# An attention and feed-forward kernel: the summaries of batches 1 to 3 turn their weights in blocks on VectorE, with one maximum for four chunks

## The chip, the core and the metric

The kernel runs on one core of a Trainium2 chip, as one launch. Its time is device microseconds of that core. Besides TensorE (matmuls and turns through the array), VectorE, ScalarE and GpSimd do the arithmetic, and SyncE (SP) issues nearly all transfers, in the order of its own queue.

## The reference

`x` is 4 batches of 12,480 tokens with 128 channels, `inducing` 32 rows of 128 channels, all in single precision. Per batch:

```python
def mab(q, kv):
    s = scale * (q @ kv.transpose(0, 2, 1))      # scale = 1/sqrt(128)
    s = s - s.max(-1, keepdims=True)
    a = np.exp(s)
    a /= a.sum(-1, keepdims=True) + 1e-09
    return a @ kv
h = mab(I, x)          # the summary: 32 rows attend to 12,480 tokens
y = mab(x, h)          # every token attends to those 32 rows
# then, for all 49,920 tokens:
t = y @ w_in           # 128 -> 2048
g = where(t >= 1, t, where(t <= -1, 0, (t + 1)**2 / 4))
out = g @ w_out        # 2048 -> 128
```

## The kernel before

A batch is cut into 26 chunks of 480 tokens. For every chunk, `chunk` makes the 2048 hidden rows in eight steps of two 128-row halves: TensorE writes them to PSUM (line 953), ScalarE takes relu(t+1) (line 961) and then its square over 4 (line 947), VectorE the smaller of that and max(t, 1) (line 966). In six of eight steps the result is split into a rounded part `hi` and a rest `lo`, and TensorE adds three products (line 1053); `hi` is made by VectorE, ScalarE or GpSimd, whichever the plan picks, and `lo` by GpSimd (line 1027). In the other two one product in full precision does. VectorE turns the chunk's output (line 1065), and SP stores it in four pieces.

Before a batch's chunks can start, its 32 summary rows must be known. `summarize(b)` makes them. Batch 0's runs at the start, with nothing beside it; those of batches 1 to 3 run beside the chunks of the batch before. A summary works on groups of four chunks: six full ones and one of two. For a group of batches 1 to 3:

- `load` fetches `xn`, 120 partitions by 4 rows of tokens for each chunk, from a pool of nine buffers, and `xr`, the same tokens in 32-wide pieces, which VectorE turns into `xT` (channels by tokens).
- `score`: four matmuls, one for each chunk, write to the four 32-row quadrants of one PSUM bank (line 554): row 32q + m has the scores of summary row m with the tokens of chunk q. VectorE takes each row's maximum (line 559) and its multiple by -scale (line 562), ScalarE the exponentials with their sum (line 571). The bank is held from the first of these steps to the last.
- `gather`: TensorE turns the weights, four transposes of 120 tokens each, into another bank (line 595); ScalarE or VectorE copies them to `eN` (line 603). Then 16 matmuls (line 611) weigh the tokens: quadrant q of the output takes weights and tokens of chunk q only, so each quadrant stands under its own maximum. ScalarE keeps the result in `hs` (line 618).

After the last group, small steps bring the 28 partial sums of each summary row under one maximum, and add them with matmuls over `hs` (line 694). The maxima and sums of each group and quadrant stand in `mg` and `sg`.

All work is put in order by a planner in the file, `Plan.order`. Each operation is added with an engine or a choice of engines, a cost and a lag in nanoseconds, and a due time; the plan runs a clock, and whenever an engine is free it takes the operation that could start and is due first. The operations are then issued in that order, so each engine and SP's queue have a fixed order. Buffers, PSUM banks among them (pool `h`, seven banks), are given out by the plan as well. `DUE`, `LONE`, `KEEP` and `WAIT` are its constants: `LONE` puts off an operation whose twin (the other half of a step) isn't ready, since both halves in neighbouring banks can be done by one wide operation.

Of the kernel before, what the change touches and what calls it, by code (L numbers as in the profile page):

```python
# [9 lines left out]
F32 = mybir.dt.float32  # L10
# [3 lines left out]
ALU = mybir.AluOpType  # L14
# [9 lines left out]
SLOTS = dict(  # L24
    h=7, o=1, xn=9, xT=26, xr=2, e1=1, eN=1, hw=6, hx=1, hy=1, w=8, hi=4, lo=4, aT=3, s2=2, a=1, ahi=1, oT=1
)

FIRST = ["xn", "w", "xn", "hi", "xn", "w", "xn", "lo", "xn", "w"]

# [3 lines left out]
DUE = {  # L33
# [17 lines left out]
    "end": [-102350],  # L51
# [18 lines left out]

LONE = {"r": 7750, "t": 3200}

KEEP = 100

WAIT = 175250

# [176 lines left out]
def attn_moe(  # L253
# [29 lines left out]

    SHAPE = [(5, 96)] + [(4, 120)] * (B - 1)
    x_first = x.rearrange("b (k p t) c -> b k p t c", p=96, t=5)
    x_rows = x.rearrange("b (k t p) c -> b k p t c", p=120, t=4)
# [3 lines left out]
    FORM = dict(  # L290
        xn=([96, 5, C], F32), xT=([C, CW], F32),
        xr=([C, NB, M], F32), e1=([P, CW], F32), eN=([96, 5, P], F32), hw=([P, 512], F32R), hx=([P, 512], F32R), hy=([P, 512], F32R),
        w=([P, 2, CW], F32), hi=([P, 2, CW], F32R), lo=([P, 2, CW], F32R), aT=([P, CW], F32R),
        s2=([P, NB, M], F32), a=([P, CW], F32), ahi=([P, CW], F32R), oT=([C, NB, M], F32),
    )
    banks = psum.tile([P, SLOTS["h"] + SLOTS["o"], 512], F32, name="banks")
    count = [0]

    def make(slot, shape=None, dtype=None):

        count[0] += 1
        if slot.pool in ("h", "o"):
            slot.tile = banks[:, slot.place + (SLOTS["h"] if slot.pool == "o" else 0), :]
            return slot.tile
# [17 lines left out]
    def in_turn(pool, near=None):  # L322
        turns[pool] += 1
        return Slot(pool, turns[pool] - 1, near)
# [162 lines left out]
    def summarize(b, begin, pace, end):  # L487

        xn, got, e1, eN = {}, {}, {}, {}
        T, TP = SHAPE[b]  # L490
        rows_of = x_rows if b else x_first
        lasts, mosts, summed = [], [], []
        prior = state.get("chain")

        def load(g, due, step):
            for q in range(nqs[g]):
                c = g * Q + q
                due += step
                xT[b, c] = in_turn("xT")

                pool = FIRST[c % len(FIRST)] if b == 0 else "xn"
                xn[c] = in_turn(pool) if pool == "xn" else Slot(pool)
                got[c] = add(
                    "SP", 700 if b else 1000, 3000 if b else 5800, at(due, "x") if b else at(0, "x0", c),
                    lambda c=c: nc.sync.dma_start(make(xn[c], [TP, T, C], F32), rows_of[b, c]), [], [xn[c]],
                )
                got_all[b, c] = got[c]
                if b == 0:
                    pt = Slot("h")

                    def turn(c=c, pt=pt):
                        p = make(pt)
                        for t in range(T):
                            nc.tensor.transpose(  # L514
                                p[:, t * TP : (t + 1) * TP], xn[c].tile[:, t, :], ident[:TP, :TP]
                            )

# [25 lines left out]
        def score(g, due):  # L543

            nq = nqs[g]
            rows = nq * M
            cs = [g * Q + q for q in range(nq)]
            p1, e1[g] = Slot("h"), Slot("e1")
            nb = small("nb", [P, 1], f"_{b}_{g}")

            def scores():
                p = make(p1)
                for q, c in enumerate(cs):
                    nc.tensor.matmul(  # L554
                        p[q * M : (q + 1) * M, :CW], indT, xT[b, c].tile, start=True, stop=True
                    )

            def most():
                nc.vector.tensor_reduce(
                    mg[:rows, g : g + 1], p1.tile[:rows, :CW], axis=AX.X, op=ALU.max  # L560
                )
# [16 lines left out]
            v = add("DVE", 760, 900, SC[1], most, [m, folded, prior], [p1])  # L578
            mosts.append(v)
            e = add("ACT", 645, 780, SC[2], exps, [v], [e1[g], p1])  # L580
            summed.append(e)
            return e

        def gather(g, due, scored):
# [3 lines left out]
            pe, pf, ph, eN[g] = Slot("h"), Slot("h"), Slot("h"), Slot("eN")  # L588
            to = [pe, pf] if b == 0 else [pe]

# [9 lines left out]
            def put():  # L600
                copy = nc.scalar.copy if v.engine == "ACT" else nc.vector.tensor_copy
                e = make(eN[g], [TP, T, P], F32)
                copy(e[:, :4, :rows], pe.tile[:TP].rearrange("p (t w) -> p t w", w=P)[:, :, :rows])  # L603
                if b == 0:
                    copy(e[:, 4, :rows], pf.tile[:TP, :rows])

# [12 lines left out]

            GA = [at(due, "GA", n) for n in range(4)] if b else [at(0, "g0", g)] * 4  # L620
# [3 lines left out]
            by = dict(DVE=(615, 750, when), ACT=(485, 620, when))  # L624
            if b == 0:
                by = dict(ACT=(660, 800, when) if nq == Q else (430, 570, when))
            v = add(by, 0, 0, 0, put, [m], [eN[g], *to])
# [510 lines left out]
```

## Time and profile before

| | us |
|---|---|
| median of 3 runs | 1732.59 (1731.34 to 1733.43) |
| profiled execution | 1732.11 |
| its span, first to last instruction | 1730.3 |
| TensorE busy (matmuls) | 1696.6 |
| ScalarE busy | 1664.2 |
| VectorE busy | 1626.2 |
| GpSimd busy | 1612.6 |

Busy time is the time in which at least one instruction of the engine ran. A matmul's end is modelled, so a busy TensorE may still have room. The granted clock of TensorE was 0.999 of full speed. A row of groups reads: line, engine, operation, what it writes and reads, shapes, count, then busy time, mean duration, and idle time before.

### The profile page before, as it was taken

The numbers are of one execution on the slowest core, as the hardware profiler recorded it, in microseconds if no ns is written. First come the engines' busy times: TensorE is split into PE (matmuls) and PEld (weight loads), VectorE is DVE, ScalarE is ACT, GpSimd is POOL, SyncE is SP. The second block draws the span as 40 slices with busy tenths as digits, with TensorE's granted clock in tenths as the row PEclk, the third lists the DMA queues.
The fourth block names the chain that finished last, engine by engine and source line by source line (L and its number), as shares of the span: only waits on it lengthen the run. The fifth ranks groups of instructions, "written<-read, shape, count | busy, mean of one in ns | idle before, by whom it ended". The sixth has DMA issues, their size and how long they took to land.

```text
span 1730.3 us, 26049 instructions
## 1 busy us (share of the span) xinstructions
PE 1696.6 (98%) x8062; PEld 1229.5 (71%) x8062; DVE 1626.2 (94%) x2167; ACT 1664.2 (96%) x2486; POOL 1612.6 (93%) x875
## 2 busy tenths in 40 slices
PE   6999999999999999999999999999999999999998
PEld 5667777777767777777777777777777677777776
DVE  5799999999999999999999999999999999999997
ACT  5699999999999999999999999999999999999997
POOL 1599999999899999999999999999989999999997
PEclk9999999999999999999999999999999999999999
DMA  9443323333334233343143333232212111111111
GB/s 235 112 74 69 74 58 70 57 62 61 70 66 77 47 72 63 66 75 68 31 93 54 74 68 69 51 66 52 42 34 53 33 30 30 35 35 35 33 31 18
DMA packets 427950, 105.76 MB, mean 61 GB/s; under 512 B 370562, under 2 KB 421218, under 8 KB 427810
## 3 DMA queue, kind: packets, MB, share of 16 engines
q1 hardware_dynamic: 426722, 103.84, 30.5%
q8 instruction: 64, 1.05, 0.3%
q14 instruction: 76, 0.62, 0.1%
q10 hardware_dynamic: 1088, 0.25, 0.1%
HBM read 48.94 MB, written 25.56 MB: 43 GB/s over the span
## 4 chain that ended last, share of the span: by engine, by line
PE 62%; ACT 16%; DVE 11%; issue 5%; POOL 3%; DMA 2%; SPq 1%; DVEq 0%; ACTq 0%; POOLq 0%
PE banks L1053 43%; PE banks L953 14%; ACT w L961 8%; ACT w L947 6%; DVE w L966 6%; DVE hi L1024 3%; POOL lo L1027 2%; PE banks L611 1%; PE banks L765 1%; ACT hi L1021 1%; PE banks L554 1%; SPq L532 1%; DMA xr<-in_x 1%; DVE oT L1065 1%; PE banks L514 1%
## 5 line engine op out<-in xcount | busy, mean ns | idle before, releaser
L1027 POOL TENSOR_TENSOR lo<-w,hi 128x960 fp32r<-128x960 f32 x623 | 1395.9, 2271 | 40.3 <-DVE hi L1024 17.9
L966 DVE SCALAR_TENSOR_TENSOR w<-banks,w 128x480 f32<-128x480 f32 (+1 forms) x1200 | 960.6, 838 | 35.9 <-ACT w L947 30.7
L961 ACT ACTIVATE w<-banks 128x480 f32<-128x480 f32 (+1 forms) x1352 | 843.7, 700 | 15.0 <-PE banks L953 13.9
L947 ACT ACTIVATE w<-w 128x960 f32<-128x960 f32 x832 | 842.2, 1049 | 2.7
L953 PE MATMUL banks<-aT,hw 128*128 128x480 f32 x1664 | 605.6, 432 | 7.3 <-DVE w L966 5.2
L1053 PE MATMUL banks<-hi,w_lo 128*128 128x480 f32 x1246 | 492.0, 395 | 5.4 <-DVE oT L1065 3.3
L1024 DVE TENSOR_REDUCE hi<-w 128x960 fp32r<-128x960 f32 x409 | 464.7, 1142 | 18.2 <-PE banks L1053 1.2
L1053 PE MATMUL banks<-hi,w_hi 128*128 128x480 f32 x1246 | 472.9, 380 | 0.0
L953 PEld LDWEIGHTS banks<-aT,hw 128*128 128x128 f32 x1664 | 304.7, 188 | 167.6 <-DVE w L966 71.1
L1053 PE MATMUL banks<-w,w_f 128*128 128x480 f32 x836 | 391.4, 567 | 0.0
L1053 PE MATMUL banks<-lo,w_hi 128*128 128x480 f32 x1246 | 385.2, 395 | 0.8 <-POOL lo L1027 0.8
L1053 PEld LDWEIGHTS banks<-hi,w_lo 128*128 128x128 f32 x1246 | 234.2, 188 | 76.2 <-DVE oT L1065 18.0
L1053 PEld LDWEIGHTS banks<-lo,w_hi 128*128 128x128 f32 x1246 | 229.8, 188 | 76.2 <-POOL lo L1027 25.7
L1053 PEld LDWEIGHTS banks<-hi,w_hi 128*128 128x128 f32 x1246 | 234.2, 188 | 40.0 <-issue 7.2
L1053 PEld LDWEIGHTS banks<-w,w_f 128*128 128x128 f32 x836 | 155.9, 189 | 68.7 <-issue 50.9
L1019 POOL TENSOR_SCALAR hi<-w 128x960 fp32r<-128x960 f32 x140 | 139.6, 1002 | 19.3 <-DVE w L966 10.4
L1021 ACT CAST hi<-w 128x960 fp32r<-128x960 f32 x74 | 75.5, 1021 | 4.7 <-DVE w L966 3.1
L1065 DVE STREAM_TRANSPOSE oT<-banks 128x480 f32<-128x480 f32 x104 | 70.1, 674 | 7.9 <-PE banks L1053 6.5
L535 DVE STREAM_TRANSPOSE xT<-xr 128x480 f32<-128x480 f32 x78 | 51.2, 659 | 0.0
L808 POOL TENSOR_TENSOR a<-a,ahi 128x480 fp32r<-128x480 f32 (+1 forms) x28 | 34.5, 1232 | 0.6 <-ACT ahi L805 0.6
L441 POOL TENSOR_TENSOR w_in_sb<-hi,lo 128x256 f32<-128x256 f32 x8 | 6.1, 763 | 28.4 <-DVE hi L430 28.4
L611 PEld LDWEIGHTS banks<-xn,eN 120*32 120x32 f32 (+1 forms) x754 | 24.4, 109 | 11.1 <-ACT eN L603 4.4
(107 smaller groups left out, 580.0 us busy)
## 6 DMA issues: line engine op xcount, KB each, us to landing
out<-oT SPq DMA_DIRECT2D x414, 60.0 KB, 2.2
xn<-in_x SPq DMA_DIRECT2D x91, 240.0 KB, 4.2
xr<-in_x SPq DMA_DIRECT2D x312, 60.0 KB, 2.5
aT<-ahi SPq DMA_DIRECT2D x206, 60.0 KB, 2.0
aT<-a SPq DMA_DIRECT2D x206, 60.0 KB, 2.0
w<-in_moe_w_in SPq DMA_DIRECT2D x8, 256.0 KB, 5.7
w<-in_moe_w_out SPq DMA_DIRECT2D x8, 256.0 KB, 3.8
hw<-hy SPq DMA_DIRECT2D x32, 64.0 KB, 2.0
```

Of the source, the lines that this page charges most:

```text
L535: nc.vector.transpose(make(xT[b, c]), xr.tile.rearrange("c n i -> c (n i)"))
L611: nc.tensor.matmul(p[q * M : (q + 1) * M, :C], eN[g].tile[:, t, q * M : (q + 1) * M], xn[g * Q + q].tile[:, t, :], start=(t == 0), stop=(t ...
L947: nc.scalar.activation(w.tile, w.tile, AF.Square, scale=0.5)
L953: nc.tensor.matmul(make(h)[:, :CW], hw[b][ft // 4].tile[:, ft % 4 * P : (ft % 4 + 1) * P], aT[b, c].tile, start=True, stop=True,)
L961: each(of, i, hs_, lambda h, to: nc.scalar.activation(to, h, AF.Relu, bias=1.0), w)
L966: lambda h, t: nc.vector.scalar_tensor_tensor(h if kept else t, h, 1.0, t, op0=ALU.max, op1=ALU.min), w,
L1019: nc.gpsimd.tensor_scalar(make(hi), w.tile, 1.0, 0.0, op0=ALU.mult, op1=ALU.add)
L1021: nc.scalar.copy(make(hi), w.tile)
L1024: nc.vector.tensor_reduce(make(hi), w.tile.unsqueeze(3), axis=AX.X, op=ALU.max)
L1027: nc.gpsimd.tensor_sub(make(lo), w.tile, hi.tile.bitcast(F32))
L1053: nc.tensor.matmul(acc.tile[:, :CW], wt[k][:, i, :], g.tile[:, i, :], start=first, stop=(acc.parts == 0),)
L1065: nc.vector.transpose(make(oT).rearrange("c n i -> c (n i)"), acc.tile[:, :CW])
```

## The change

For batches 1 to 3 alone:

- The tokens for weighing are loaded like `xr`'s, 32 partitions by 15 consecutive tokens for a chunk, and the four chunks of a group share one buffer, a quadrant each. The buffers are three, of 15 x 128 columns over all partitions; batch 0 uses the same memory as nine buffers of 96 partitions. The first load of a later batch waits for the weighing of batch 0.
- The maximum of each row goes to `mq`; four transfers bring the four quadrants' maxima side by side on 32 partitions, VectorE takes the maximum over them, and four transfers write it to all quadrants of `mg`. So the four chunks stand under one maximum.
- The exponentials are written in the order in which the scores lie.
- Instead of TensorE's turns and the copy, one VectorE instruction turns all 32 x 32 blocks of `e1` into `eN`. Block n then has, for every quadrant, 32 tokens by 32 summary rows.
- 15 matmuls weigh the tokens, each over the 128 partitions of the four chunks together; matmul n adds to quadrant n % 4.

Batch 0 keeps its instructions. All due times but those of the weights and of batch 0's loads, turns, scores and weighing are new, and so are `LONE`, `KEEP` and `WAIT`.

```diff
-LONE = {"r": 7750, "t": 3200}
-KEEP = 100
-WAIT = 175250
+LONE = {"r": 6200, "t": 800}
+KEEP = 800
+WAIT = 210850
...
+                    xn[c] = xn[c - 1] if q else in_turn("xn")
+                    def fetch(c=c, q=q):
+                        t = xn[c].tile or make(xn[c])
+                        nc.sync.dma_start(t[q * M : (q + 1) * M], x_cols[b, c])
+                    got[c] = add("SP", 700, 3000, at(due, "x"), fetch, state["first"], [xn[c]])
...
             def most():
-                nc.vector.tensor_reduce(
-                    mg[:rows, g : g + 1], p1.tile[:rows, :CW], axis=AX.X, op=ALU.max
-                )
+                to = mq[:rows] if b else mg[:rows, g : g + 1]
+                nc.vector.tensor_reduce(to, p1.tile[:rows, :CW], axis=AX.X, op=ALU.max)
+                if b == 0:
+                    less()
+            def line(q):
+                nc.sync.dma_start(m4[:, q : q + 1], mq[q * M : (q + 1) * M])
+            def one_most():
+                nc.vector.tensor_reduce(m4[:, Q:], m4[:, :nq], axis=AX.X, op=ALU.max)
+            def spread(q):
+                nc.sync.dma_start(mg[q * M : (q + 1) * M, g : g + 1], m4[:, Q:])
+            def less():
                 nc.vector.tensor_scalar(nb[:rows], mg[:rows, g : g + 1], -SCALE, None, op0=ALU.mult)
...
-                    to = make(e1[g])[:rows].rearrange("w (i n) -> w i n", i=M)
-                    of = p1.tile[:rows, :CW].rearrange("w (n i) -> w i n", i=M)
+                    to, of = make(e1[g])[:rows], p1.tile[:rows, :CW]
...
+                l = [add("SP", 610, 2700, SC[1], lambda q=q: line(q), [v]) for q in range(nq)]
+                v = add("DVE", 75, 215, SC[1], one_most, l)
+                l = [add("SP", 610, 2700, SC[1], lambda q=q: spread(q), [v, prior]) for q in range(Q)]
+                mosts.extend(l)
+                v = add("DVE", 75, 215, SC[1], less, l)
...
+            if b:
+                def over():
+                    to = make(eN[g], [P, NB, M])[:rows].rearrange("p n m -> p (n m)")
+                    nc.vector.transpose(to, e1[g].tile[:rows])
+                def weigh_all():
+                    p = make(ph)
+                    for n in range(NB):
+                        nc.tensor.matmul(
+                            p[n % Q * M : (n % Q + 1) * M, :C], eN[g].tile[:rows, n, :], xn[g * Q].tile[:rows, n, :],
+                            start=n < Q, stop=n >= NB - Q,
+                        )
+                def keep_all():
+                    nc.scalar.copy(hs[:, g, :], ph.tile[:, :C])
+                v = add("DVE", 600, 735, GA[1], over, [scored], [e1[g], eN[g]])
+                m = add("PE", 880, 1080, GA[2], weigh_all, [v, *(got[g * Q + q] for q in range(nq))],
+                        [ph, eN[g], xn[g * Q]], tiled=True)
+                lasts.append(add("ACT", 150, 290, GA[3], keep_all, [m, folded, prior], [ph]))
+                return
```

## Rows read from the trace of the kernel before

**Rows 1.** The page's head and engine table: busy us, share of the span.

```profile
span 1730.3 us, 26049 instructions
PE 1696.6 (98%) x8062; PEld 1229.5 (71%) x8062; DVE 1626.2 (94%) x2167; ACT 1664.2 (96%) x2486; POOL 1612.6 (93%) x875
```

**Rows 2.** The page's chain that ended last, by engine.

```profile
PE 62%; ACT 16%; DVE 11%; issue 5%; POOL 3%; DMA 2%; SPq 1%; DVEq 0%; ACTq 0%; POOLq 0%
```

**Rows 3.** Stretches between output turns, line 1065 alone: stretch, us, VectorE busy (count), clock.

```profile
932.60:1345.20 412.60, 17.52 (x26) 1.00 0.29 56
1345.20:1725.00 379.80, 16.88 (x25) 1.00 0.16 31
```

**Rows 4.** Stretches, all engines: us, then PE, PEld, DVE, ACT, POOL busy.

```profile
93.90:516.00 422.10, 417.39 (x1947) 300.41 (x1947) 404.41 (x523) 416.04 (x613) 407.37 (x220) 1.00 0.35 66
516.00:932.60 416.60, 414.52 (x1934) 300.18 (x1933) 399.03 (x523) 410.08 (x611) 402.04 (x216) 1.00 0.34 65
932.60:1345.20 412.60, 410.54 (x1914) 298.70 (x1913) 393.95 (x513) 406.38 (x601) 396.76 (x210) 1.00 0.29 56
1345.20:1725.00 379.80, 376.65 (x1524) 273.67 (x1523) 364.78 (x451) 372.29 (x539) 369.95 (x192) 1.00 0.16 31
```

**Rows 5.** Groups of one summary, by shape, from 500 to 900 us.

```profile
L611 PE MATMUL banks<-xn,eN 120*32 120x128 f32 x208 | 7.6, 276 | 0.0
L554 PE MATMUL banks<-xT,indT 128*32 128x480 f32 x52 | 7.1, 578 | 0.0
...
L571 ACT ACTIVATE e<-banks,nb 128x480 f32<-128x480 f32 x6 | 4.1, 683 | 0.0
L802 DVE STREAM_TRANSPOSE a<-s 128x480 f32<-128x480 f32 x6 | 4.0, 670 | 0.4 <-POOL s L797 0.4
...
L595 PE MATMUL banks<-ident,e 128*120 128x128 f32 x24 | 3.6, 272 | 0.0
...
L603 ACT COPY eN<-banks 120x512 f32<-120x512 f32 x4 | 2.5, 614 | 0.0
...
L694 PE MATMUL banks<-ff,hs 128*128 128x32 f32 x14 | 1.7, 264 | 0.0
L603 DVE COPY eN<-banks 120x512 f32<-120x512 f32 x2 | 1.4, 687 | 0.3 <-PE banks L595 0.3
...
L720 PE MATMUL banks<-w_in_sb,hT 128*32 128x512 f32 x8 | 1.1, 604 | 0.0
...
L595 PE MATMUL banks<-ident,e 64*120 64x64 f32 x4 | 0.4, 230 | 0.0
L603 DVE COPY eN<-banks 120x256 f32<-120x256 f32 x1 | 0.4, 425 | 0.4 <-PE banks L595 0.4
...
L653 DVE TENSOR_REDUCE m<-mg 128x1 f32<-128x7 f32 x1 | 0.1, 144 | 0.0
```

**Rows 6.** Timeline of one group's scores, exponentials and turns: start us, us, what.

```profile
588.66 1.01 PE L554 MATMUL banks<-xT,indT 128*32 128x480 f32 x8
...
593.10 2.61 SPq L1069 DMA_DIRECT2D out<-oT  x4
...
595.38 0.68 ACT L571 ACTIVATE e<-banks,nb 128x480 f32<-128x480 f32 x1
...
597.86 0.60 PE L595 MATMUL banks<-ident,e 128*120 128x128 f32 x4
...
598.22 0.68 PE L953 MATMUL banks<-aT,hw 128*128 128x480 f32 x2
...
600.56 0.68 DVE L603 COPY eN<-banks 120x512 f32<-120x512 f32 x1
```

**Rows 7.** Line 831, the pieces of aT: us from issue to landing.

```profile
DMA to landing us min/median/max: 1.9/2.0/3.8
```

**Rows 8.** What SP's queue waited for: us in total, times, longest us.

```profile
SPq L1069 <- DVE oT L1065: 381.9, 51, 12.3
```

**Rows 9.** Waits of the engines: us in total, times, longest us.

```profile
PEld banks L953 <- DVE w L966: 71.1, 221, 1.7
```

More of the change, by code (lines that the diff above doesn't have):

```diff
@@ L24 @@
 SLOTS = dict(
-    h=7, o=1, xn=9, xT=26, xr=2, e1=1, eN=1, hw=6, hx=1, hy=1, w=8, hi=4, lo=4, aT=3, s2=2, a=1, ahi=1, oT=1
+    h=7, o=1, xn=3, x3=9, xT=26, xr=2, e1=1, eN=1, hw=6, hx=1, hy=1, w=8, hi=4, lo=4, aT=3, s2=2, a=1, ahi=1, oT=1
 )
-FIRST = ["xn", "w", "xn", "hi", "xn", "w", "xn", "lo", "xn", "w"]
+FIRST = ["x3", "w", "x3", "hi", "x3", "w", "x3", "lo", "x3", "w"]
 STEP = 1950
 DUE = {
[17 rows of a table removed]
-    "end": [-102350],
[17 rows of a table added]
+    "end": [-87250],
     "wi": [-503600, -107150, -99300, -322650, -80150, -599500, -48900, 17550],
@@ L280, in attn_moe @@
     psum = ctx.enter_context(tc.tile_pool(name="psum", bufs=1, space=bass.MemoryType.PSUM))
-    SHAPE = [(5, 96)] + [(4, 120)] * (B - 1)
+    T, TP = 5, 96
     x_first = x.rearrange("b (k p t) c -> b k p t c", p=96, t=5)
-    x_rows = x.rearrange("b (k t p) c -> b k p t c", p=120, t=4)
     x_cols = x.rearrange("b (k i n) c -> b k i n c", i=M, n=NB)
@@ L290, in attn_moe @@
     FORM = dict(
-        xn=([96, 5, C], F32), xT=([C, CW], F32),
+        xT=([C, CW], F32),
         xr=([C, NB, M], F32), e1=([P, CW], F32), eN=([96, 5, P], F32), hw=([P, 512], F32R), hx=([P, 512], F32R), hy=([P, 512], F32R),
@@ L296, in attn_moe @@
     banks = psum.tile([P, SLOTS["h"] + SLOTS["o"], 512], F32, name="banks")
+    tokens = work.tile([P, SLOTS["xn"], 3 * 5 * C], F32, name="tokens")
     count = [0]
@@ L303, in make @@
             slot.tile = banks[:, slot.place + (SLOTS["h"] if slot.pool == "o" else 0), :]
+            return slot.tile
+        if slot.pool == "xn":
+            slot.tile = tokens[:, slot.place, :].rearrange("p (n c) -> p n c", n=NB)
+            return slot.tile
+        if slot.pool == "x3":
+            n, k = divmod(slot.place, 3)
+            slot.tile = tokens[:TP, n, k * T * C : (k + 1) * T * C].rearrange("p (t c) -> p t c", t=T)
             return slot.tile
@@ L489, in summarize @@
         xn, got, e1, eN = {}, {}, {}, {}
-        T, TP = SHAPE[b]
-        rows_of = x_rows if b else x_first
         lasts, mosts, summed = [], [], []
         prior = state.get("chain")
+        state.setdefault("first", lasts)
         def load(g, due, step):
@@ L499, in load, with fetch @@
                 xT[b, c] = in_turn("xT")
[L501 to L505, printed above, removed]
-                )
+                if b == 0:
+                    pool = FIRST[c % len(FIRST)]
+                    xn[c] = in_turn(pool) if pool == "x3" else Slot(pool)
+                    def fetch(c=c):
+                        nc.sync.dma_start(make(xn[c], [TP, T, C], F32), x_first[b, c])
+                    got[c] = add("SP", 1000, 5800, at(0, "x0", c), fetch, [], [xn[c]])
+                else:
+                    xn[c] = xn[c - 1] if q else in_turn("xn")
[3 more added lines that the diff above has]
+                    got[c] = add("SP", 700, 3000, at(due, "x"), fetch, state["first"], [xn[c]])
                 got_all[b, c] = got[c]
@@ L513, in turn @@
                         for t in range(T):
-                            nc.tensor.transpose(
-                                p[:, t * TP : (t + 1) * TP], xn[c].tile[:, t, :], ident[:TP, :TP]
-                            )
+                            nc.tensor.transpose(p[:, t * TP : (t + 1) * TP], xn[c].tile[:, t, :], ident[:TP, :TP])
                     def put(c=c, pt=pt):
@@ L549, in score @@
             nb = small("nb", [P, 1], f"_{b}_{g}")
+            mq, m4 = small("mq", [P, 1], f"_{b}_{g}"), small("m4", [M, Q + 1], f"_{b}_{g}")
             def scores():
@@ L577, in score @@
                     [p1, e1[g], *(xT[b, c] for c in cs)], tiled=True)
-            v = add("DVE", 760, 900, SC[1], most, [m, folded, prior], [p1])
-            mosts.append(v)
+            v = add("DVE", 760 if b == 0 else 690, 900, SC[1], most, [m, folded, prior], [p1])
+            if b == 0:
+                mosts.append(v)
+            else:
+                l = [add("SP", 610, 2700, SC[1], lambda q=q: line(q), [v]) for q in range(nq)]
[3 more added lines that the diff above has]
+                v = add("DVE", 75, 215, SC[1], less, l)
             e = add("ACT", 645, 780, SC[2], exps, [v], [e1[g], p1])
@@ L588, in gather @@
             pe, pf, ph, eN[g] = Slot("h"), Slot("h"), Slot("h"), Slot("eN")
-            to = [pe, pf] if b == 0 else [pe]
+            if b:
[11 more added lines that the diff above has]
+                    nc.scalar.copy(hs[:, g, :], ph.tile[:, :C])
+                GA = [at(due, "GA", n) for n in range(4)]
+                v = add("DVE", 600, 735, GA[1], over, [scored], [e1[g], eN[g]])
[3 more added lines that the diff above has]
+                return
+            to = [pe, pf]
             def turn():
@@ L603, in put @@
                 copy(e[:, :4, :rows], pe.tile[:TP].rearrange("p (t w) -> p t w", w=P)[:, :, :rows])
-                if b == 0:
-                    copy(e[:, 4, :rows], pf.tile[:TP, :rows])
+                copy(e[:, 4, :rows], pf.tile[:TP, :rows])
             def weigh():
@@ L618, in keep @@
                 nc.scalar.copy(hs[:rows, g, :], ph.tile[:rows, :C])
-            GA = [at(due, "GA", n) for n in range(4)] if b else [at(0, "g0", g)] * 4
+            GA = [at(0, "g0", g)] * 4
             each_ = 110 if nq == Q else 85
@@ L623, in gather @@
             when = GA[1]
-            by = dict(DVE=(615, 750, when), ACT=(485, 620, when))
-            if b == 0:
-                by = dict(ACT=(660, 800, when) if nq == Q else (430, 570, when))
+            by = dict(ACT=(660, 800, when) if nq == Q else (430, 570, when))
             v = add(by, 0, 0, 0, put, [m], [eN[g], *to])
```

2 lines of the change are left out of this document (1 added, 1 removed), and 48 rows, old and new, of the table DUE.

## The prediction

> **What bounds the kernel now.** I read the engine table first. TensorE is busy 98% of the span of 1730.3 us, ScalarE 96%, VectorE 94%, GpSimd 93% [rows 1]: four engines near their ends, so the table alone doesn't choose. The chain that ended last does: 62% of it lies on TensorE, 16% on ScalarE, 11% on VectorE, 3% on GpSimd, 1% on SP's queue [rows 2].
>
> Then I compare stretches. The change touches the summaries of batches 1 to 3, which run beside the chunks of batches 0 to 2; beside batch 3 there is none. Counted from output turn to output turn, batch 2 takes 412.6 us for 26 chunks, and batch 3 takes 379.8 us for 25, 15.19 us each, so 395.0 us for 26 [rows 3]; batch 1 takes 416.6 us [rows 4]. A summary thus costs (416.6 + 412.6)/2 - 395.0 = 19.6 us. TensorE's own work for one is 7.6 (weighing) + 7.1 (scores) + 3.6 + 0.4 (turning the weights) + 1.7 + 1.1 (the end of the summary) = 21.5 us [rows 5]. So a summary costs what TensorE does for it, at 19.6/21.5 = 0.91 us per us; what it asks of the other engines lies beside that.
>
> A rule speaks against this reading: the Trainium skill, in "Perfetto Trace Analysis", section "Identifying the Most-Contended Engine", says that the busy share of matmuls is no good measure of nearness to the limit, and takes the share of weight loads for TensorE and occupancy for the others. By it TensorE stands at 71% and ScalarE, at 96%, would be the bound. Rows 3 to 5 speak for TensorE; what the time would be by the other reading is the second rival.
>
> **The change part by part.**
>
> *Turns leave TensorE.* Gone are 24 + 4 transposes per later batch, 3.6 + 0.4 = 4.0 us busy [rows 5], 12.0 us over three batches. Busy time has the end of the pipeline in it: a group of four starts at 597.86 and the next matmul at 598.22, 0.36 us, against 0.60 busy [rows 6]; six such groups and half a one make 2.3 us a batch, 7 in all. That is the lower end, 12.0 the upper. By the price above I take 0.91 x 12.0 = 10.9.
>
> *Weighing.* 16 matmuls per full group become 15; the trace has two instructions for each (208 for a batch's six full groups and one half one, at 7.6 us). So 32 take 1.17 us, and two fewer save 0.07, 18 times 1.2 us. The half group goes from 16 instructions to 30, four quadrants at a time where there were two; its length should stay. Bounds 0 and 2; 1.2 taken. TensorE's sum: 12.1.
>
> *VectorE's turn for the copy.* The copies out of PSUM go: per batch 4 on ScalarE, 2.5 us, and 2 and a half one on VectorE, 1.4 + 0.4 us [rows 5]; ScalarE loses 7.5 us in all, VectorE 5.4. VectorE gains 21 SBUF-to-SBUF block turns; the nearest row, of the same shape, is the turn of a at 0.670, so 14.1. The maximum over the four chunks is a new small operation; the nearest row is the 7-column reduction, 0.144, so 21 x 0.144 = 3.0. Net 11.7 more on VectorE. In batches 0 to 2 it is idle 422.1 - 404.4 + 416.6 - 399.0 + 412.6 - 394.0 = 53.9 us [rows 4], which covers it. At the chain's shares this is +11.7 x 0.11 = 1.3 and -7.5 x 0.16 = -1.2: 0.1. With the cover gone it costs all 11.7.
>
> *The exponentials* no longer read PSUM in another order: 0.683 now, 0.614 for the plain copy of the nearest shape [rows 5]. Between 0 and 21 x 0.07 = 1.4 us of ScalarE; 0 taken.
>
> *The common maximum goes through SP.* Each group adds 4 transfers that bring four maxima side by side and 4 that send the result back, 168 in all. An issue takes about 0.65 us (2.61 for four [rows 6]): 109 us of SP. Per four chunks, some 64 us, SP now issues 16 stores, 16 pieces of aT, 16 loads of xr and 4 of xn, some 34 us, so there is room. But SP takes its queue in order: an issue that waits for a maximum holds back the stores, the pieces of aT and the loads behind it, and TensorE would miss aT first. SP already stands still 381.9 us in 51 waits for output turns [rows 8], and the view of waits has no row where TensorE waits for a transfer of aT. I price it at nothing; if that cover fails, each of the 21 maxima that SP waits for through one operation of VectorE (0.67 for a turn [rows 5]) costs that: 14 us.
>
> *What the round trips hold.* From scores through maxima to exponentials a bank of PSUM is held, in one group now from 588.66 to 596.06, 7.4 us, and the turned weights' own bank from 597.86 to 601.24, 3.4 more, 10.8 together [rows 6]; without waits it would be 1.01 + 0.67 + 0.14 + 0.68 for the first (the maxima priced by the turn of the same shape and the small reduction [rows 5, 6]) and 0.60 + 0.68 for the second, 3.8. After: 1.8 to the end of the maxima, twice three issues and a landing (3 x 0.65 + 2.0 = 4.0 [rows 6, 7]), 0.3 for two small operations and 0.7 for the exponentials, 10.8 us, more where SP is busy; the second bank is not needed. So 0 to 7 us more, 4 taken; 21 times, 84 us in which six banks serve the chunks where seven did. Weight loads wait 71.1 us for a bank that VectorE frees [rows 9], 4.3% of the time; doubled in those 84 us, 3.7. Much of that lies under a running matmul (98% busy to the loads' 71% [rows 1]): 0 to 3.7, 1 taken.
>
> *Waits at the head of VectorE's queue*, two per group, 42. Behind a waiting instruction stand the bounds of the chunks, which free banks. Pieces of aT land after 2.0 us as a median, 3.8 at most [rows 7]; were one in ten a microsecond late, 4 us. Bounds 0 and 42; 2 taken.
>
> *Loads of x for weighing* come as 32 runs of 15 rows where they came in single rows; a shorter transfer that is issued ahead of use: nothing. That they wait for the last weighing of batch 0 holds only loads that have a batch's time. Batch 0's summary keeps its instructions, in other buffers: nothing.
>
> *Due times.* Nearly all others are new, and no row prices them. The fullest engine beside TensorE, ScalarE, is idle 6.5 of 416.6 us in batch 1 and 7.5 of 379.8 in batch 3 [rows 4]: an order alone can hardly win more than 28 us, and as much could be lost. I take 0, and 6 either way.
>
> Sum: -12.1 + 0.1 + 1 + 2 = -9.0 from the profiled execution's 1732.11 us, of which 1730.3 is the span: 1723.1. The median shown, 1732.59, lies 0.5 higher: **1723.6**.
>
> **The rivals.**
>
> *The due times win more than the structure*: half of ScalarE's gap in three batches, 10 us more, 1714. For it: the gaps are there. Against: they recur under four full engines.
>
> *Another engine is the bound, and the gain lies beside it.* By the rule above, ScalarE, VectorE and GpSimd share the chunk work (hi goes to whichever is free), and their sum rises by 11.7 - 7.5 = 4.2 us, 1.4 each: 1734, no change. For it: ScalarE is busy 410.08 of 416.6 us in batch 1 [rows 4]. Against: in batch 3 the three run at 98, 96 and 97% with no summary beside them, and a summary costs what TensorE's rows say.
>
> *VectorE waits for maxima that come late through SP*: slower. The place is the head of VectorE's queue, 42 times. If SP is caught in another four issues, 2.6 us, at each, VectorE loses 109 us, has 53.9 - 11.7 = 42 to spare, and the kernel takes 67 us more less 12: 1788. It decides from an average lateness of (42 + 12)/42 = 1.3 us; at 1.5 the time is 1741. For it: SP's long waits in order. On queues the Trainium skill ("DMA: Bandwidth & Descriptors", section "Queues, rings and completion order") says that each DMA engine consumes descriptors in ring order, so a small transfer follows a bulky one. The trace agrees so far as landings of one kind spread from 1.9 to 3.8 us [rows 7]. Against: the bulky loads come in fewer pieces, and only the last of four landings counts.
>
> *Weighing doesn't run four quadrants at a time* with 128 rows: 30 instructions at the 0.09 us of a turn [rows 6] make 2.7 us where there is 1.1, 21 x 1.6 = 34 us, 1758. Against: scores, with 128 rows and 32 columns, do overlap: 8 of 0.578 us in 1.01 us [rows 5, 6].
>
> **How the numbers follow.** The forecast (1717 to 1729) has 0.56; the due times 0.14; another engine 0.15; late maxima 0.11; no overlap 0.04. Below 1729.1, which is 0.2%, about what a measurement can tell from no change, lie the first two, 0.70; within 0.2% the third, 0.15; above it the rest, 0.15. The range 1712 to 1738 leaves out a part of the second case, most of the fourth and all of the fifth, under 0.2.
>
> **What would show it.** Right: no transposes on TensorE beside batches 0 to 2; the period of batches 1 and 2 down from 414.6 by 3 to 4 us, batch 3's at 395 within 3; weighing at 1.0 to 1.1 us a group; VectorE some 4 us busier a batch and hardly ever released by a DMA. Wrong: periods that stand still while VectorE waits for DMAs above 15 us; weight loads' waits for banks well above 71 us; batch 3 or the first 94 us, where no structure changes, moving more than the rest.

## The result, and the profile after

The changed kernel takes 1735.01 us (median of 20 runs, 1733.70 to 1737.20), the kernel before 1732.20 beside it (20 runs): a ratio of 1.0017 [1.0010, 1.0023]. It is slower by 0.17%, where 1723.6 was forecast. Its profiled execution took 1734.02 us, of which 1732.2 is the span.

The first reading is the page's engine table and the shares of its chain, which answer to [rows 1, 2].

```profile
span 1732.2 us, 26108 instructions
...
PE 1693.1 (98%) x7994; PEld 1221.9 (71%) x7994; DVE 1625.6 (94%) x2178; ACT 1662.4 (96%) x2450; POOL 1613.9 (93%) x876
...
PE 70%; DVE 11%; ACT 9%; issue 4%; POOL 2%; DMA 1%; SPq 1%; DVEq 0%; POOLq 0%; ACTq 0%
```

Hardly anything moved: TensorE is 3.5 us less busy, the three elementwise engines together 4901.9 us against 4903.0. The second reading is by stretch, from output turn to output turn (columns as in [rows 4]).

```profile
100.90:519.50 418.60, 414.97 (x1906) 298.31 (x1907) 398.35 (x530) 412.63 (x605) 399.76 (x214) 0.99 0.35 67
519.50:934.50 415.00, 412.56 (x1908) 296.19 (x1907) 399.62 (x526) 409.66 (x592) 402.67 (x216) 1.00 0.34 65
934.50:1349.10 414.60, 412.39 (x1908) 296.95 (x1908) 396.56 (x515) 408.43 (x585) 400.75 (x214) 1.00 0.28 54
1349.10:1727.10 378.00, 375.69 (x1523) 272.77 (x1522) 364.59 (x451) 369.47 (x540) 370.84 (x193) 1.00 0.16 31
```

The stretches beside [rows 4] are 3.5, 1.6, -2.0 and 1.8 us shorter, 4.9 in all. Batches 1 and 2, where the changed structure runs from end to end, take 829.6 us for 829.2: nothing. The first output turn comes at 100.9 instead of 93.9. So -4.9 and +7.0 leave about +2, the span's 1.9. The two don't separate cleanly: VectorE, ScalarE and GpSimd did 9.8 us less in the four stretches (4743.1 to 4733.3) but only 1.1 less in the whole span, so 8.7 us of their work now stands before the first output, 2.9 for each.

The third reading is of the start. These are windows of 5 us of the kernel after (last columns: granted clock, share of the DMA engines, GB/s), and below them the same of the kernel before.

```profile
75.00:80.00 5.00, 2.27 (x8) 1.42 (x8) 3.65 (x6) 4.88 (x8) 3.01 (x4) 1.00 0.45 86
95.00:100.00 5.00, 3.04 (x12) 1.75 (x10) 3.50 (x4) 4.65 (x9) 5.00 (x4) 1.00 0.50 94
100.00:105.00 5.00, 3.44 (x9) 2.88 (x10) 4.74 (x8) 3.51 (x5) 3.68 (x3) 0.55 0.84 186
105.00:110.00 5.00, 5.00 (x19) 3.99 (x17) 3.85 (x7) 3.97 (x6) 4.03 (x2) 0.77 0.20 46
```

```profile
75.00:80.00 5.00, 4.70 (x18) 2.94 (x17) 4.12 (x7) 4.90 (x8) 4.84 (x5) 1.00 0.54 84
95.00:100.00 5.00, 3.54 (x14) 2.11 (x13) 4.04 (x5) 4.96 (x9) 5.00 (x4) 1.00 0.49 94
100.00:105.00 5.00, 5.00 (x21) 3.66 (x20) 5.00 (x8) 4.90 (x8) 4.09 (x3) 1.00 0.50 97
```

TensorE loses 2.4 us at 75 to 80 and idles again ahead of 100. The chain of waits of the kernel after shows what the first output waits for (start, us, what).

```profile
94.15 0.59 SPq L887
94.74 0.05 issue
94.83 0.59 SPq L547
95.47 0.62 SPq L547
96.09 0.04 issue
96.14 0.63 SPq L547
96.81 0.62 SPq L547
97.43 0.04 issue
97.48 0.62 SPq L887
98.14 2.04 DMA aT<-a
100.22 0.05 issue
100.26 0.68 DVE a L858
100.94 0.57 DVE oT L1121
101.56 0.77 PE banks L1109
```

SP issues four loads of `xr` (L547) before the last piece of `aT` (L887); VectorE's turn of the next `a` waits until that piece has been read out of the buffer; and the first output's turn stands behind it in VectorE's queue. In the kernel before, the first output's turn came 3.8 us ahead of that turn of `a` (93.91 and 97.68).

The fourth reading is of one changed group: what the summary's rows cost, from 500 to 900 us, as in [rows 5], and the timeline of one group, as in [rows 6].

```profile
L634 PE MATMUL banks<-tokens,eN 128*32 128x128 f32 x180 | 6.4, 275 | 0.0
...
L629 DVE STREAM_TRANSPOSE eN<-e 128x480 f32<-128x480 f32 x6 | 3.9, 658 | 0.0
...
L634 PE MATMUL banks<-tokens,eN 64*32 64x128 f32 x30 | 1.1, 272 | 0.0
...
L585 DVE TENSOR_REDUCE m<-m 32x1 f32<-32x4 f32 x6 | 0.8, 128 | 0.3 <-DMA m<-mq 0.3
```

```profile
590.02 1.01 PE L570 MATMUL banks<-xT,indT 128*32 128x480 f32 x8
...
594.66 2.41 SPq L582 DMA_DIRECT2D m<-mq  x4
...
599.91 0.10 DVE L585 TENSOR_REDUCE m<-m 32x1 f32<-32x4 f32 x1
...
602.72 2.47 SPq L588 DMA_DIRECT2D mg<-m  x4
...
608.68 0.14 DVE L591 TENSOR_SCALAR nb<-mg 128x1 f32<-128x1 f32 x1
...
611.26 0.69 ACT L599 ACTIVATE e<-banks,nb 128x480 f32<-128x480 f32 x1
```

The new operations cost what was forecast: a block turn 0.658 (0.670 taken), the one maximum 0.128 (0.144). The weighing takes 6.4 + 1.1 us a batch for 7.6, so 0.3 us less over three batches where 1.2 was taken. The bank of this group is held twice as long as forecast, from 590.02 to 611.95. Over the 21 groups of batches 1 to 3 it is held 17.5 us on average, from the first score to the end of the exponentials; in the kernel before it was 5.0, and 2.7 more for the bank of the turned weights. The group from which the prediction took its 10.8 us held them longer than most. These are the waits of the kernel after beside [rows 8, 9] (engine, line, releaser: us, times, longest).

```profile
PEld banks L1009 <- DVE w L1022: 64.7, 209, 0.8
...
DVE a L858 <- DMA aT<-a: 2.2, 3, 1.8
...
DVE m L585 <- DMA m<-mq: 0.3, 1, 0.3
```

### The profile page after: what moved, and what is told of

It is laid out like the page before. It is cut to its first block, busy times and chain, and to the rows that moved or that the text cites. A ratio compares the mean times of both kernels' runs of the same rounds, so it can differ in the third digit from the quotient of the medians.

```text
span 1732.2 us, 26108 instructions
## 1 busy us (share of the span) xinstructions
PE 1693.1 (98%) x7994; PEld 1221.9 (71%) x7994; DVE 1625.6 (94%) x2178; ACT 1662.4 (96%) x2450; POOL 1613.9 (93%) x876
## 4 chain that ended last, share of the span: by engine, by line
PE 70%; DVE 11%; ACT 9%; issue 4%; POOL 2%; DMA 1%; SPq 1%; DVEq 0%; POOLq 0%; ACTq 0%
PE banks L1109 50%; PE banks L1009 16%; DVE w L1022 6%; ACT w L1017 4%; ACT w L1003 3%; DVE hi L1080 3%; POOL lo L1083 2%; PE banks L634 1%; PE banks L821 1%; PE banks L570 1%; DVE oT L1121 1%; PE banks L1138 0%; DMA ind_sb<-in_inducing 0%; DMA w<-in_moe_w_out 0%; SPq L547 0%
## 5 line engine op out<-in xcount | busy, mean ns | idle before, releaser
L1009 PE MATMUL banks<-aT,hw 128*128 128x480 f32 x1664 | 586.4, 422 | 6.6 <-DVE w L1022 5.4
L1109 PE MATMUL banks<-hi,w_lo 128*128 128x480 f32 x1246 | 519.4, 417 | 9.9 <-DVE oT L1121 5.7
L1080 DVE TENSOR_REDUCE hi<-w 128x960 fp32r<-128x960 f32 x404 | 458.2, 1141 | 12.6 <-PE banks L1109 1.4
L1009 PEld LDWEIGHTS banks<-aT,hw 128*128 128x128 f32 x1664 | 305.6, 188 | 151.9 <-DVE w L1022 64.7
L1109 PE MATMUL banks<-lo,w_hi 128*128 128x480 f32 x1246 | 409.1, 402 | 1.5 <-POOL lo L1083 1.5
L1109 PEld LDWEIGHTS banks<-lo,w_hi 128*128 128x128 f32 x1246 | 230.6, 188 | 80.8 <-issue 26.4
L570 PE MATMUL banks<-xT,indT 128*32 128x480 f32 x208 | 28.7, 586 | 0.0
```

Of the source, the lines that this page charges most:

```text
L570: nc.tensor.matmul(p[q * M : (q + 1) * M, :CW], indT, xT[b, c].tile, start=True, stop=True)
L1009: nc.tensor.matmul(make(h)[:, :CW], hw[b][ft // 4].tile[:, ft % 4 * P : (ft % 4 + 1) * P], aT[b, c].tile, start=True, stop=True,)
L1080: nc.vector.tensor_reduce(make(hi), w.tile.unsqueeze(3), axis=AX.X, op=ALU.max)
L1109: nc.tensor.matmul(acc.tile[:, :CW], wt[k][:, i, :], g.tile[:, i, :], start=first, stop=(acc.parts == 0),)
```

## The experiments

Theory A is the prediction's: TensorE sets the time of the chunks, at 0.91 us per us, and something took the gain back. Theory B is its second rival: the chunks go by the elementwise engines, so the gain was never there. Theory C: the due times, new or unfit, decide. The times of all runs stand against the kernel before on the same chip (medians 1732.2 to 1732.7); where no kernel is named, the edit is to that kernel, whose order of instructions stays.

### Structure and due times

**The turns cut from the kernel before** (three of four left out).

```diff
-                for t in range(T):
+                for t in range(3 if b else 0, T):
```

> The kernel before in its own order, with three of the four turns of each later group left out (54 + 9 of 84 transposes; the copy reads old data in their place, so the weights are wrong). If TensorE bounds the chunks, as the prediction had it, three quarters of 7 to 12 us go: 5 to 9 us faster than before, 1.7 to 3 us per batch in batches 0 to 2 and none in batch 3. If another engine bounds them, the time stays within 1.5 us of before.

1731.26 us, ratio 0.9988 [0.9978, 0.9998]; stretches 421.0, 416.5, 412.5 and 379.5. Three quarters of the turns are worth about 1 us, not 8. This already speaks against A: nothing was added that could take a gain back.

**The kernel after without its round trips** (the four transfers, the maximum over them and the four transfers back are empty; each quadrant stands under its own maximum).

```diff
-                nc.sync.dma_start(m4[:, q : q + 1], mq[q * M : (q + 1) * M])
+                pass
...
-                nc.vector.tensor_reduce(m4[:, Q:], m4[:, :nq], axis=AX.X, op=ALU.max)
+                pass
```

> The changed kernel in its own order, with the eight transfers of each later group, the maximum over the chunks and so the common maximum left out: every quadrant keeps its own maximum, as before (the sums are then wrong). If the round trips through SP cost the gain (held bank, waits at VectorE's head), the time falls by 4 us or more under the changed kernel, in batches 0 to 2. If they are free, it stays within 1.5 us of the changed kernel.

1736.57 us, 1.0019 [1.0009, 1.0030]. The first output comes at 103.25, 2.4 us later than in the kernel after; from there to the last output both take 1626.2 us. So in this order of instructions the 168 transfers and the waits for them at the head of VectorE's queue cost nothing that can be measured: the third rival (late maxima) falls. What the long hold of the bank costs is not shown by this run. The exponentials keep their place in ScalarE's queue, and the bank is held as long as with the transfers (the group shown above, and 17.5 us on average here too):

```profile
591.12 1.01 PE L570 MATMUL banks<-xT,indT 128*32 128x480 f32 x8
...
612.37 0.70 ACT L599 ACTIVATE e<-banks,nb 128x480 f32<-128x480 f32 x1
```

**The structure after with the due times and constants of before.**

```diff
-LONE = {"r": 6200, "t": 800}
-KEEP = 800
+LONE = {"r": 7750, "t": 3200}
+KEEP = 100
...
```

> The changed structure with the due times, LONE, KEEP and WAIT of the kernel before. If the new due times lose the 7 us up to the first output (93.9 to 100.9 us), the first output comes back to within 2 us of 94 and the time lies 3 us or more under before's. If the structure loses them (loads of batch 1 held until the weighing of batch 0 ends), the first output stays 4 us or more late and the time doesn't fall under before's.

1745.73 us, 1.0075 [1.0054, 1.0095]; first output at 97.7, stretches 426.6, 419.2, 413.9 and 380.5.

**The structure before with the due times and constants of after** (the same lines the other way).

> The structure before with the new due times, LONE, KEEP and WAIT. If the new due times lose the start, the first output comes 4 us or more after 93.9 us here too and the time is 3 us or more over before's. If the structure does, the first output stays within 2 us of 93.9. Batches 0 to 2 show what the due times alone do to a period (416 us on the mean of batches 0 to 2).

1755.73 us, 1.0126 [1.0106, 1.0146]; first output at 99.2, stretches 420.2, 424.7, 422.9 and 382.1. Neither swap brings back the first output of the kernel before (93.9): the new due times alone put it at 99.2, the new structure alone at 97.7. The structure after is 11 us worse under the other's constants, the structure before 23. So the two halves of the change can't be priced apart by swapping them: each order is fitted to its structure, and swapping measures the misfit. Theory C in its simple form, that the new constants are better or worse by themselves, isn't borne out.

### Work added to one engine

Nothing is left out in these three; the work is made once more, and its result is the same.

```diff
-                for t in range(T):
+                for t in [*range(T)] * (2 if b else 1):
```

> The kernel before in its own order, with the turns of each later group made twice on TensorE (84 more transposes, 7 to 12 us of TensorE; the result is the same). If TensorE is the bound at 0.91 us per us, the time rises by 6 to 11 us. If ScalarE is (98.5% busy beside the chunks), it rises by under 2 us, as leaving the turns out gained next to nothing.

1739.91 us, 1.0044 [1.0031, 1.0056]: +7.6, as much as 21 x 0.36 us from start to start [rows 6].

```diff
+                    nc.scalar.copy(to, of)
```

> The kernel before in its own order, with one copy of 128 x 480 from PSUM more on ScalarE ahead of each later group's exponentials (21 times about 0.6 us, 11 to 13 us of ScalarE; the result is the same). If ScalarE is the bound, the time rises by 8 to 13 us. If TensorE is, by under 4 us.

1742.83 us, 1.0061 [1.0049, 1.0074]: +10.5 for 21 copies of some 0.59 us.

```diff
+                for _ in range(2 if b else 1):
                     nc.vector.tensor_reduce(
```

> The kernel before in its own order, with the maximum of each later group taken twice on VectorE (21 times 0.65 us, 13 us of VectorE; the result is the same). It stands for the 11.7 us that the change adds to VectorE. If VectorE's 54 us of idle time cover it, as the prediction had it, the time rises by under 3 us. If VectorE is one of the bounds, by 6 to 13 us.

1743.47 us, 1.0065 [1.0053, 1.0078]: +11.1 for 21 maxima of some 0.65 us. Work added to any one of the three costs 0.8 to 1.0 us per us (for TensorE by the time from start to start; by the 12.0 us of busy time it is 0.6). No work was added to GpSimd. VectorE's 53.9 us of idle time [rows 4], which the prediction let cover its added turns, covers little (2.5 of 13.6 us) for an instruction put into a fixed order.

### The start

**The kernel after with the first loads of batch 1's tokens issued later.** Seven of them stand in SP's queue from 57 to 62 us, in the middle of the start; here the first twelve are issued one by one behind loads of `xr`.

```diff
+                        held.append(go)
+                        if not (b == 1 and g < 3):
+                            while held:
+                                held.pop(0)()
...
+                        if k == Q - 1 and held:
+                            held.pop(0)()
```

> The changed kernel in its own order, but for the first twelve token loads of batch 1: seven of them went out at 57 to 62 us, just ahead of the spreading of hw; here they follow one by one behind later loads of xr. If that burst delays the start, the first output comes 2 us or more earlier than with the changed kernel (100.9 us) and the time falls by as much. If the order of the engines' own work does, the first output stays within 1 us of it.

1737.40 us, 1.0030 [1.0019, 1.0040]; the first output comes at 104.6, which is 3.7 us later, not earlier. Moving the burst of loads wins nothing back.

**The kernel after with one due time moved**: the scores of the sixth group of the first summary, whose maximum VectorE took at 52.62 us, 2.56 later than in the kernel before, behind conversions of `w_out`.

```diff
-    "s0": [-544850, -216450, -295450, -187350, -468800, -106350, -463400],
+    "s0": [-544850, -216450, -295450, -187350, -468800, -600000, -463400],
```

> The changed kernel with one due time changed: the scores, maximum and exponentials of batch 0's sixth group come first (s0 entry 5 from -106350 to -600000). In the changed kernel VectorE converts w_out pieces ahead of that group's maximum (52.62 us, 50.06 before) and TensorE's first summary ends at 63.7 us. If this order loses the start, the maximum comes at 49 us or earlier, the summary ends 3 us or more sooner (60.7 or earlier), the first output comes by as much sooner, and the time falls 3 to 6 us under the changed kernel's, to the level of before or under it. If the start is lost elsewhere (transfers, clock), the first output moves by under 1.5 us.

1731.88 us, 0.9994 [0.9985, 1.0003], where the kernel after has 1.0017. The first summary is done at 59.4 instead of 63.7 us (61.3 in the kernel before), the first output at 98.5 instead of 100.9.

**The kernel after with other due times for the weights' conversions and the first summary's scores and weighing** (`wc`, `oc`, `s0`, `g0`).

> The changed kernel with new due times for the first phase alone (scores and weighing of batch 0, conversions of the weights; nothing of the chunks or of later batches). If the gain beside the chunks is there (4.9 us from first to last output in the two profiles) and only the start hides it, the first output comes at 95 us or earlier and the time is 3 us or more under before's: it beats both. If the start can't be had with the changed structure, it stays over before's.

1732.14 us, 0.9996 [0.9987, 1.0005]; first summary 58.4, first output 98.1. Both starts give back a part of the 7 us, 2.4 and 2.8, and the loss against the kernel before is gone; neither is faster than it. Their first summary ends 1.9 and 2.9 us earlier than in the kernel before, and yet the first output comes 4.6 and 4.2 us later, so what is left of the loss lies between the two. There VectorE idles 2.8 and 2.7 us ahead of the same turn of `a`. That the order of SP's queue costs these 4 us is read from the chain; it wasn't tried by itself.

### Work taken away in small

**Later maxima over 96 of the 480 columns** (the other columns' scores are not looked at).

```diff
-                    mg[:rows, g : g + 1], p1.tile[:rows, :CW], axis=AX.X, op=ALU.max
+                    mg[:rows, g : g + 1], p1.tile[:rows, : 96 if b else CW], axis=AX.X, op=ALU.max
```

> The kernel before in its own order, with the maxima of the later groups taken over the first 96 of 480 columns (some 8 us less of VectorE in 21 groups; the maxima are then too small). If VectorE has room to spare, as the prediction had it, or if every engine stands at its limit and the others keep the time, it stays within 1.5 us of before. If VectorE is the one bound, it falls by 5 us or more.

1732.65 us, 1.0000 [0.9991, 1.0009]; VectorE is busy 1619.9 us where 1626.2 was.

**That, the turns cut and the exponentials without their sums, together.**

```diff
+                if b:
+                    nc.scalar.activation(to, of, AF.Exp, bias=nb[:rows], scale=SCALE)
...
+                for t in range(3 if b else 0, T):
```

> The kernel before in its own order, with three things left out of the later groups at once: three of four turns on TensorE, the maxima beyond 96 columns on VectorE, and the sums that ScalarE reads out behind the exponentials (21 times about 0.22 us; the results are then wrong). If the engines are at their limits together, so that one engine's saving alone shows nothing (1.2 us for the turns), the three together give more than the sum of turns and maxima alone, 4 us or more. If there is room on them all, it stays within 2 us of before.

1730.82 us, 0.9989 [0.9980, 0.9998]. Adding costs nearly its whole length, taking away gives next to nothing, on TensorE, on VectorE, and on both with a little of ScalarE. GpSimd was cut in none of them, and all the cuts were small; the next four make them large.

### Work taken away at scale, in the chunks of batches 1 to 3

**TensorE alone.**

```diff
+                            n = 360 if b and len(terms) == 1 and wt is w_hi else CW
                             nc.tensor.matmul(
-                                acc.tile[:, :CW], wt[k][:, i, :], g.tile[:, i, :],
+                                acc.tile[:, :n], wt[k][:, i, :], g.tile[:, i, :n],
```

> The kernel before in its own order; in batches 1 to 3 the products of w_hi with lo go over 360 of the 480 columns (the other columns are left out of the sum). Products start 0.215 us apart, so a quarter of each of 936 is some 50 us less for TensorE, nothing less for the other engines. If TensorE paces the chunks at the 0.91 us per us of the prediction: 1687. If the three elementwise engines pace them, or all four together: 1727 to 1732.

1725.61 us, 0.9960 [0.9947, 0.9972]: -7.1 for 50 us (936 products that take 0.165 us from start to start where 0.218 was), 0.14 us per us. A forecasts -45.

**GpSimd** (with 10 us of TensorE).

```diff
-                    nc.gpsimd.tensor_sub(make(lo), w.tile, hi.tile.bitcast(F32))
+                    n = 456 if b else CW
+                    nc.gpsimd.tensor_sub(make(lo)[:, :, :n], w.tile[:, :, :n], hi.tile.bitcast(F32)[:, :, :n])
```

> The kernel before in its own order; in batches 1 to 3 GpSimd's lo and the products that read it cover 456 of the 480 columns (the last 24 are left out). lo takes 2271 ns for 960 columns, so 48 columns fewer are 0.11 us, 468 times: some 53 us less for GpSimd, and 10 for TensorE. If GpSimd alone binds in the fixed order: 1685 to 1690. If TensorE paces: 1723. If all four bind together: 1727 to 1732.

1728.02 us, 0.9972 [0.9962, 0.9982]: -4.7, with GpSimd busy 1567.8 us where 1612.6 was. GpSimd doesn't bind alone either.

**The three elementwise engines.**

```diff
-                nc.scalar.activation(w.tile, w.tile, AF.Square, scale=0.5)
+                n = 456 if b else CW
+                nc.scalar.activation(w.tile[:, :, :n], w.tile[:, :, :n], AF.Square, scale=0.5)
...
-                            h if kept else t, h, 1.0, t, op0=ALU.max, op1=ALU.min
+                            *(v[..., : 456 if b else CW] for v in (h if kept else t, h)), 1.0,
+                            t[..., : 456 if b else CW], op0=ALU.max, op1=ALU.min
```

> As the run on GpSimd's lo, and ScalarE's square and VectorE's bound of batches 1 to 3 cover 456 of 480 columns as well (the last 24 are left out there): some 53 us less for GpSimd, 32 for ScalarE (1049 ns for 960, 624 times), 30 for VectorE, 10 for TensorE. If the three elementwise engines pace the chunks and TensorE has room: 1697 to 1705. If TensorE paces: 1723. If all four bind together: 1720 to 1732.

1714.58 us, 0.9895 [0.9879, 0.9910]: -18.2, under B's -27 to -35. Of the 115 us planned (53, 32 and 30), the page shows 95 (GpSimd 46.6, ScalarE 21.8, VectorE 27.0 against [rows 1]):

```profile
PE 1678.2 (98%) x8062; PEld 1234.9 (72%) x8062; DVE 1599.2 (93%) x2167; ACT 1642.4 (96%) x2486; POOL 1566.0 (91%) x875
```

**All four** (both edits).

> As the run with all three elementwise engines cut, and the products of w_hi with lo over 360 columns: TensorE 50 us less, GpSimd 53, ScalarE 32, VectorE 30. If all four engines bind together, so that only a cut of each of them is a cut of the time: 1695 to 1705, where each of the cuts alone gives under 10. If the time goes by one of them alone, this gives what that one's run gives.

1701.84 us, 0.9826 [0.9812, 0.9839]: -30.9, nearly the whole of the smallest cuts (30 and 32 us by plan, 30.8 and 26.4 by the page, on VectorE and ScalarE). The 40 us of TensorE that this cuts beyond the run before are worth 12.7 here.

```profile
PE 1661.6 (98%) x8062; PEld 1203.0 (71%) x8062; DVE 1595.4 (94%) x2167; ACT 1637.8 (96%) x2486; POOL 1565.2 (92%) x875
```

Batch 1 (second stretch) with TensorE alone cut, with the three cut, and with all four cut:

```profile
515.10:929.30 414.20, 409.52 (x1934) 288.89 (x1933) 398.18 (x524) 409.15 (x611) 401.44 (x216) 1.00 0.34 65
```

```profile
517.00:927.00 410.00, 408.16 (x1934) 302.09 (x1933) 390.11 (x524) 402.35 (x611) 386.71 (x216) 1.00 0.34 66
```

```profile
515.50:921.50 406.00, 402.80 (x1934) 291.08 (x1933) 388.82 (x523) 400.98 (x611) 386.32 (x216) 1.00 0.35 67
```

VectorE, ScalarE and GpSimd together fill 97.3%, 95.9% and 96.6% of their time in these three, 96.9% in the kernel before [rows 4] and 97.3% in the kernel after. What this shows: neither TensorE nor GpSimd paces the chunks alone, and TensorE's time is worth 0.32 us per us once the other three are cut as well, 0.14 before. The three without TensorE's 40 us give 18.2, and those 40 us at 0.14 would add 5.6; together they give 30.9, 7 more than that sum. Neither VectorE nor ScalarE was cut alone at this size, so whose work gave the 18.2 is not shown; that one of them alone sets the time is spoken against by the 12.7 us that TensorE's cut adds while they stay the same. That all four pace the chunks together, in a fixed order, is the reading that fits these runs best.

## Why the prediction was wrong

**The price of TensorE's time, 0.91 us per us, was the step that failed first.** The chain, with 62% on TensorE [rows 2], chose the engine; the price was worked out from the 19.6 us that a summary costs beside 21.5 us of TensorE's work. The same rows fit another price. The three elementwise engines together are busy (1211.2 + 1197.1)/2 = 1204.1 us in batches 1 and 2 and 1107.0 x 26/25 = 1151.3 in batch 3's measure [rows 4]; a summary thus asks 52.8 of them, 17.6 each, and at 97% full that is 18.1. A slope between stretches that differ in the work of every engine can't say whose work it prices. That second price isn't shown either: cut together by 31.8 us each on average, the three gave 18.2. Cut alone, TensorE's time is worth 0.14: the 12.0 us of turns would give 1.7 where 10.9 was taken, and the run with the turns cut gave about 1.

**TensorE's 98% says little of nearness to its end.** The prediction counted TensorE among four engines near their ends and chose it by the chain and the stretches. With some 50 us of its work gone, the page of that run still has 98%, and its busy time fell by 15:

```profile
PE 1681.6 (98%) x8062; PEld 1196.6 (69%) x8062; DVE 1624.6 (94%) x2167; ACT 1661.5 (96%) x2486; POOL 1610.9 (94%) x875
```

A matmul's end is modelled, and other matmuls show longer busy times in that run: the first products (line 953) 618.3 us where 605.6 was. The Trainium skill ("Perfetto Trace Analysis", section "Identifying the Most-Contended Engine") says that the busy share of matmuls is no good measure, and the prediction weighed that and decided against it. The run agrees with the rule. The section's advice to optimize the engine of highest occupancy first, here ScalarE with 96%, was tried by no run; cut together with VectorE and GpSimd it gave 18, and it took TensorE's cut too to reach 31.

**The rival that "another engine is the bound, and the gain lies beside it" had the place and the time (1734), but not the mechanism whole.** It added 4.2 us to the elementwise engines; measured is -1.1 over the span. The largest lines of VectorE and ScalarE, before and after:

```profile
L966 DVE SCALAR_TENSOR_TENSOR w<-banks,w 128x480 f32<-128x480 f32 (+1 forms) x1200 | 960.6, 838 | 35.9 <-ACT w L947 30.7 <-PE banks L1053 2.0 <-issue 0.8
L961 ACT ACTIVATE w<-banks 128x480 f32<-128x480 f32 (+1 forms) x1352 | 843.7, 700 | 15.0 <-PE banks L953 13.9
L947 ACT ACTIVATE w<-w 128x960 f32<-128x960 f32 x832 | 842.2, 1049 | 2.7
```

```profile
L1022 DVE SCALAR_TENSOR_TENSOR w<-banks,w 128x480 f32<-128x480 f32 (+1 forms) x1182 | 958.5, 849 | 43.3 <-ACT w L1003 37.7 <-POOL lo L1083 1.7 <-POOL hi L1075 1.4
L1017 ACT ACTIVATE w<-banks 128x480 f32<-128x480 f32 (+1 forms) x1325 | 840.0, 701 | 16.3 <-PE banks L1009 13.2 <-POOL lo L1083 1.0 <-issue 0.5
L1003 ACT ACTIVATE w<-w 128x960 f32<-128x960 f32 x832 | 838.4, 1037 | 4.0
```

The three lines lose 2.1, 3.7 and 3.8 us, the first two with fewer instructions (more of them wide ones, for both halves of a step), the third with shorter ones. So the new order won back on the chunks what the structure added; that is read from these sums, no run shows it alone. After the first output the forecast's sum of -9.0 came out at -4.9, and that in batches 0 and 3, while 1 and 2, where it was to be seen, stood still.

**The start was priced at nothing, and it costs 7.0 us at the first output.** "Batch 0's summary keeps its instructions" holds, but their order doesn't: with more conversions of `w_out` in front of a maximum, and attends of the second group in front of the first output, the same instructions take longer. Of the 7.0, 2.4 us are there when the first summary is done (61.3 and 63.7 us), the rest comes after that. The prediction named this as a sign of being wrong, the first 94 us moving more than the rest. Due times at 0, 6 either way, had the size; the sum had no term for the first 94 us by themselves. These two misses, 7.0 and 4.1 with the first output as the border, make the 11 us between forecast and result.

**What held**: the durations of the new operations; the round trips at nothing (0.3 us of VectorE's waits where 2 were taken, and their removal gains nothing); overlap of four quadrants in the weighing; the loads of tokens at nothing (beside 7.7 us at the start, which the kernel before has as well, no engine waits for them in the view of waits). The hold of the bank was mis-sized: 17.5 us on average where 10.8 was worked out. Weight loads wait 64.7 us where 71.1 was [rows 9], so no harm shows there, but no run shortens the hold.

**Open**: which waits of the fixed order make a cut worth 0.1 and an addition 0.8 to 1.0; that the order stays fitted to the longer work is the reading, and no run planned the order anew for the cut work. Open too are the price of ScalarE or VectorE cut alone, of the bank's hold, and of SP's order at the start.

## What to carry to other kernels

Where four engines are over 93% busy and their order is fixed, don't price a saving on one of them by the chain of waits or by the slope between stretches: cut that engine's work by a few per cent in a run of its own, and take the price in that order from it. Here an addition cost most of its length and a saving on one engine a small part of it, so an edit that moves work from one full engine to another should be priced on the sum over all of them. A new order is part of such a change: look at the start by itself, where the same instructions in another order cost 7.0 us and the rest of the edit won 4.9. And check that a run which takes something out takes out what it is meant to test: without the round trips the bank was held as long as with them.

## What was not expected of the hardware

- In the kernel after, the granted clock falls after TensorE has idled ahead of the first output: it is 0.55 and then 0.77 in the windows 100 to 105 and 105 to 110 us, which comes to 6.8 us at 1.2 GHz and, by an estimate, at most 3.4 us of TensorE's work. In the kernel before it stays at 1.00, 2.4 GHz. With the one due time moved it is 0.92 from 95 to 100 and 0.74 from 100 to 105, 3.4 us at 1.2 GHz, and the stretch of batch 0 takes 418.2 us for 418.6: the longer fall is not seen in the time.
- Transfers of one column of 32 rows (0.1 KB) between partitions take 0.59 us to issue and land 1.7 us after it as a median, 3.5 at most on the way together; the pieces of `aT`, 60 KB, take 2.0 [rows 7].
